# Expert blocks of different sizes, taken in falling order of tokens

## The chip, the cores and the metric

One NeuronCore of a Trainium2 chip runs the whole program. It has five engines with a queue each: PE (matrix multiply), DVE (vector), ACT (scalar and activation), POOL and SP. SP and ACT also issue the DMA transfers spoken of here. Each queue runs in the order written, and an instruction that waits for a semaphore holds up everything behind it on its engine. The metric is the device time of one execution in microseconds (us).

## What is computed

Three stages follow one another: a clustered attention (2 batches, 8 heads, 768 positions), a mixture of eight experts of which each token uses one, and a dense two-layer stage. The change is in the expert stage:

```
logits = x @ w_gate                        # x: 1536 x 512
expert_idx = argmax(logits, axis=1)        # one of 8 experts per token
for e in range(8):
    mask = expert_idx == e
    h = maximum(x[mask] @ w1[e], 0)        # 512 -> 1024
    out[mask] = gate_w[mask] * (h @ w2[e]) # 1024 -> 512
```

How many tokens an expert gets depends on the data. With the reference's inputs (its default seed) the counts are 198, 119, 169, 188, 162, 192, 206 and 302 for experts 0 to 7, worked out from the reference.

## The kernel before

The attention stage ends by scattering each token's row (512 numbers, its index and its gate) to a DRAM buffer `Xs`, which has a region of 1536 rows for each expert. Before that, SP fills the first rows of each region with zeros (line 687), so that a block may be read past its last token.

The expert stage runs in *blocks*. Block `blk` below 8 is expert `blk` with a fixed 208 rows (`CAP`), whatever its count. A ninth block of 128 rows (`OB`) takes the first rows that some expert has beyond 208; a table made on DVE at run time says which expert, which rows and where to put them (`table_a` to `table_e`). Any further such blocks run in a loop at lines 1049 to 1081, whose number of turns is a value read from SBUF. With the counts above, expert 7 alone has more than 208 rows (94 more), so the ninth block is used and the loop makes no turn.

A block is eight steps `f`, and a global step is `g = 8*blk + f`. In each step PE runs four matmuls of the first layer, `l1` (line 895), and four of the second, `l2` (line 911), the latter two steps behind (`LAG`). A group of four such products is eight instructions in the trace, since each 32-bit product is split in two; rows of the timeline show them as x8. The rows of the block are the moving operand, so a matmul's length grows with the rows of its block, and the weights of an expert are loaded in any case. ACT evacuates each `l1` group with a Relu (line 897) into `h`, and two PSUM banks alternate between the groups of `l1`: `l1` of step g+2 needs the Relu of step g to be done.

Each expert's weights are four chunks of 1 MB. A ring of four SBUF slots holds them, and SP issues the next block's chunk when the last matmul that reads its slot has run (`wload`, lines 126 to 131). The next block's rows are loaded from `Xs` by ACT (`x_load`, line 814) at f = 0, and PE turns them (`x_transp`, line 878) at f = 6, two quarters of the 512 columns to a PSUM bank; ACT and DVE copy the banks out.

Beside this runs the *conversion* of the third stage's weights from 64-bit to pairs of 32-bit halves: 32 pieces, each loaded by SP (0.5 MB into one of two `raw` buffers, line 150) and passed through ACT (`cv`, line 154), DVE (lines 159 to 162), ACT (line 169) and DVE (line 172). One conversion step (`conv_run`) does one part for each of five neighbouring pieces: ACT's part on piece k-1 waits for the load issued in the step before, and the load of piece k waits until DVE has consumed piece k-2. `conv_steps` decides in which global steps this happens: 22 of them spread evenly over the 72 steps of the expert stage, and one in each step of the third stage.

The loop at line 1050 also is a meeting point: all engines wait there for each other and SP for all its transfers, before the third stage begins with `x2_split` on ACT (line 1102).

Of the kernel before, what the change touches and what calls it, by code (L numbers as in the profile page):

```python
# [10 lines left out]
F32 = mybir.dt.float32  # L11
# [10 lines left out]
P = 128  # L22
# [5 lines left out]
N = B * S  # L28
# [5 lines left out]
OB = 128  # L34
XCOLS = N + CAP
XW = DM + 2
# [10 lines left out]
C_TOK = 402  # L47
C_END = 414


def make_consts():
    c = np.zeros((P, C_END), np.float32)
    p = np.arange(P)
    c[:, C_ID:C_ID + P] = np.eye(P)
    c[:, C_TRI:C_TRI + P] = p[:, None] < p[None, :]
    same = p[:, None] // NC == p[None, :] // NC
    c[:, C_FIRST:C_FIRST + P] = np.eye(P) - NC * (same & (p[:, None] < p[None, :]))
    c[:, C_TIE8:C_TIE8 + E] = E - np.arange(E)
    c[:, C_EBASE:C_EBASE + E] = N * np.arange(E)
    isk = (p // NC) % 2 == 1  # L60
    c[:, C_ESC] = np.where(isk, NEG, 1.0)
    c[:, C_ESC + 1] = np.where(isk, -NEG, 0.0)
    c[:, C_TOK:C_TOK + NT] = (p[:, None] + P * np.arange(NT)[None, :]).astype(np.int32).view(np.float32)
    return c


def make_table():


    t = np.zeros((NSEL, 3 * NOV + 1), np.float32)  # L70
# [9 lines left out]
def tile_cluster_attention_moe(ctx: ExitStack, tc: tile.TileContext, qk, kk, v, cen, cenr, gate, mw, m2w,  # L80
# [23 lines left out]
    off = const.tile([P, E], F32, name="off")  # L104
    offi = const.tile([1, E], I32, name="offi")
    ovi = const.tile([1, NSEL, 4], I32, name="ovi")


    NB = E + 1
    NCE = 4 * NB  # L110
# [3 lines left out]
    wslots, m2w_t = {}, {}  # L114
    ovr = {}
# [542 lines left out]
    for p in range(1, NPR):  # L658
# [148 lines left out]

    def halves(blk):
        return (2, CAP // 2) if blk < E else (1, OB)

    def x_load(blk, src):
        nt, np_ = halves(blk)
        xr = xrp.tile([P, 2, XW], F32, name=f"xr_{blk}", tag="xr")
        nc.scalar.dma_start(xr[0:np_, 0:nt, :], src.rearrange("(t p) d -> p t d", p=np_))
        xrt[blk] = xr
# [31 lines left out]
    placemm(rc, 0, False)  # L847
    x = xtp.tile([P, 4, CAP], F32, name="x_0", tag="x")
    for d in range(4):
# [17 lines left out]
    def x_transp(blk):  # L867
        nt, np_ = halves(blk)
        nb = nt * np_
        xr = xrt[blk]  # L870
        x = xtp.tile([P, 4, CAP], F32, name=f"x_{blk}", tag="x")[:, :, 0:nb]
        for g in range(2):
            ps = bank(2 + g)[:, 0:2 * nb]
            for k in range(2):
                d = 2 * g + k
# [3 lines left out]
            pv = ps.rearrange("p (d n) -> p d n", d=2)  # L879
            if g == 0:  # L880
                nc.scalar.activation(x[:, 0:2, :], pv, AF.Copy)
            else:
                nc.vector.tensor_copy(x[:, 2:4, :], pv)
        xts[blk] = x

    def l1(blk, f):
        nt, np_ = halves(blk)
        nb = nt * np_
        ci = 4 * blk + 2 * (f // 4)
# [12 lines left out]
    def l2(blk, f):  # L902
        nt, np_ = halves(blk)
        nb = nt * np_
        ci = 4 * blk + 2 * (f // 4) + 1
# [9 lines left out]
    def y_evac(blk, col):  # L915
        nt, np_ = halves(blk)
        nb = nt * np_
        for o, y in enumerate(yps.pop(blk)):
# [7 lines left out]
    sc = pool(moe, "sc")  # L926

    def offsets():
        t0 = sc.tile([P, E], F32, name="t0")
        t1 = sc.tile([P, E], F32, name="t1")  # L930
        nc.vector.memset(t0, 0.0)
        nc.vector.tensor_copy(t0[:, 1:E], cnt[:, 0:E - 1])
        a, bb = t0, t1
        for k, shf in enumerate((1, 2, 4)):
            dst = off if k == 2 else bb
            nc.vector.tensor_copy(dst[:, 0:shf], a[:, 0:shf])
            nc.vector.tensor_add(dst[:, shf:E], a[:, shf:E], a[:, 0:E - shf])
            a, bb = dst, a
        nc.vector.tensor_copy(offi, off[0:1, :])

# [45 lines left out]
    def table_e():  # L986
        nc.vector.tensor_scalar_add(ov[:, 2:3], ov[:, 2:3], float(N))
        nc.vector.tensor_scalar(ov[:, 3:4], sums["incl"][:, NOV - 1:NOV], -1.0, 0.0, ALU.add, ALU.max)
        nc.vector.tensor_copy(ovp, ov)
        nc.sync.dma_start(ovi, ovp)  # L990

    side = {2: [offsets], 11: [table_a], 13: [table_b], 16: [table_c], 18: [table_d], 20: [table_e]}

    def put_places(blk, c):
        nt, np_ = halves(blk)
        nc.sync.dma_start(PG[c, :].rearrange("(t p) c -> p t c", p=np_), xrt[blk][0:np_, 0:nt, DM:XW])
# [9 lines left out]

    KE = 22

    def conv_steps(g):
        if g < NG:  # L1010
            at_ = lambda g: max(0, g - 2) * KE // (NG - 2)
            return range(at_(g), at_(g + 1))
        g -= NG + LAG
        return range(KE + g, KE + g + 1) if g >= 0 else ()

    for g in range(NG + LAG):
# [11 lines left out]
        if g < NG:  # L1028
            if f == 0 and 1 <= blk + 1 < E:
                x_load(blk + 1, Xs[(blk + 1) * N:(blk + 1) * N + CAP, :])  # L1030
            if f == 2:
                if blk >= 1:
                    src = offi[0:1, blk:blk + 1] if blk < E else ovi[0:1, 0, 2:3]
                    nb = CAP if blk < E else OB
                    col[blk] = ds(reg(src, COMP, N), nb)
                    put_places(blk, ds(reg(src, [ET.SP], N), nb))
                else:
                    nc.sync.dma_start(PG[col[0], :], Xs[0:CAP, DM:XW])
                if blk + 1 == E:
                    x_load(blk + 1, Xs[ds(ovr["row"], OB), :])  # L1040
            if f == 6 and blk + 1 < NB:
                x_transp(blk + 1)
            if g == 27:
                ovr["w"] = reg(ovi[0:1, 0, 0:1], [ET.SP], 4 * (E - 1))
                ovr["row"] = reg(ovi[0:1, 0, 1:2], [ET.Activation], E * N - OB)
        conv_run(cvp, conv_steps(g))


    more = nc.values_load(ovi[0:1, 1, 3:4], min_val=0, max_val=NSEL - 1)
    with tc.For_i(0, more, 1):  # L1050
        rw = reg(ovi[0:1, 1, 0:1], [ET.SP], 4 * (E - 1))
# [11 lines left out]
        for f in range(8):  # L1063
# [138 lines left out]
def layout(inputs):  # L1202
# [7 lines left out]
    for pr in range(NPAIR):  # L1210
# [28 lines left out]
```

## Time and profile before

| | us |
|---|---|
| median of 3 runs (lowest, highest) | 747.85 (747.2, 751.29) |
| profiled execution, its own time | 746.16 |
| span of its trace | 744.4 |
| expert stage on PE, first `l1` to the end of the last `l2` | 268.97 to 471.55 |
| first matmul of the third stage | 474.87 |

The time around the span is 746.16 - 744.4 = 1.76 us. In the timeline a row is a run of like instructions on one engine: its start, its duration (until the last of them ends), and in brackets how long the engine had been idle and who released it. Matmuls overlap a little, so a group's real length is the distance between the starts of two groups and not its duration. Idle time of an engine other than the one that sets the end costs nothing by itself.

### The profile page before, as it was taken

To read this page: it belongs to the slowest core of one execution; us is meant where nothing else is said; L and a number is where in the kernel's file an instruction comes from. 1 tells how busy PE (TensorE), PEld (TensorE's weight loads), DVE (VectorE), ACT (ScalarE), POOL (GpSimd) and SP (SyncE) were. 2 spreads that over 40 slices of the span, in tenths; PEclk is the share of its full clock that TensorE was granted. 3 is DMA by queue.
4 is the path that set the end of the run, shared out by engine and by line. 5 is a ranking of instruction groups with operands and counts; after the bars stand their busy time and mean duration, and the time that the engine had idled before them with its cause. 6 is when DMAs were issued, how large, how long until landed. Compare 5 with 4: busy or idle time off the path is not lost. (4 is left out here: it accounts for less than half of the span.)

```text
span 744.4 us, 10754 instructions
## 1 busy us (share of the span) xinstructions
PE 719.0 (97%) x4102; PEld 592.5 (80%) x4102; DVE 417.2 (56%) x774; ACT 287.1 (39%) x599; POOL 64.1 (9%) x69
## 2 busy tenths in 40 slices
PE   8899999999999999999999999699999999999996
PEld 3666666666666799999999999588888888888885
DVE  6877767788876631352532425499945433544332
ACT  4867867857676312232232323333322111211111
POOL 5120120212300110000000000000002000020002
PEclk9999999999999999999999999999999999999999
DMA  9064584262530037799886977233101000010001
GB/s 295 24 198 109 215 303 104 117 166 55 139 76 1 29 110 264 217 274 250 280 265 200 306 223 251 53 113 112 58 0 57 0 1 1 0 57 1 0 1 56
DMA packets 25844, 92.74 MB, mean 125 GB/s; under 512 B 7156, under 2 KB 8703, under 8 KB 21055
## 3 DMA queue, kind: packets, MB, share of 16 engines
q1 hardware_dynamic: 20375, 75.41, 32.6%
q0 software_dynamic: 3216, 12.60, 4.9%
q10 hardware_dynamic: 2200, 4.03, 1.9%
q8 instruction: 33, 0.54, 0.3%
q14 instruction: 20, 0.16, 0.1%
HBM read 78.04 MB, written 9.74 MB: 118 GB/s over the span
## 5 line engine op out<-in xcount | busy, mean ns | idle before, releaser
L895 PE MATMUL PS<-x,w 128*128 128x208 f32 (+1 forms) x576 | 108.9, 332 | 2.2 <-ACT h L897 2.2
L911 PE MATMUL PS<-h,w 128*128 128x208 f32 (+1 forms) x576 | 108.6, 332 | 0.0
L1126 ACT ACTIVATE gh<-gg 128x512 fp32r<-128x512 f32 x48 | 30.4, 632 | 192.4 <-DVE gg L1125 192.4
L387 DVE TENSOR_REDUCE sm<-PS 128x1 f32<-128x768 f32 x96 | 91.9, 957 | 17.8 <-PE PS L381 14.3
L895 PEld LDWEIGHTS PS<-x,w 128*128 128x128 f32 x576 | 98.3, 190 | 2.4 <-ACT h L897 2.4
L397 ACT ACTIVATE P<-PS,sm 128x768 f32<-128x768 f32 x96 | 86.5, 901 | 31.6 <-DVE sm L387 31.5
L911 PEld LDWEIGHTS PS<-h,w 128*128 128x128 f32 x576 | 98.4, 190 | 0.0
L411 PEld LDWEIGHTS PS<-cst,P 128*128 128x128 f32 x576 | 63.4, 141 | 29.4 <-ACT P L397 17.3
L411 PE MATMUL PS<-cst,P 128*128 128x128 f32 x576 | 82.5, 278 | 3.1 <-ACT P L397 1.5
L1124 DVE TENSOR_SCALAR gg<-PS,alph 128x512 f32<-128x512 f32 x48 | 36.0, 750 | 78.1 <-PE PS L1116 78.1
L1114 PE MATMUL PS<-x2hi,w2h 128*128 128x512 f32 x192 | 75.5, 393 | 3.3 <-ACT x2hi L1102 3.3
L1115 PE MATMUL PS<-x2lo,w2h 128*128 128x512 f32 x192 | 75.4, 393 | 0.2 <-DVE x2lo L1103 0.2
L1116 PE MATMUL PS<-x2hi,w2l 128*128 128x512 f32 x192 | 75.4, 393 | 0.0
L1144 PE MATMUL PS<-w2l,gh 128*128 128x512 f32 x192 | 74.7, 389 | 0.0
L1145 PE MATMUL PS<-w2h,gl 128*128 128x512 f32 x192 | 74.7, 389 | 0.0
L1143 PE MATMUL PS<-w2h,gh 128*128 128x512 f32 x192 | 74.7, 389 | 0.0
L414 DVE COPY PT<-PS 128x384 f32<-128x384 f32 x96 | 53.0, 552 | 38.0 <-PE PS L411 37.9
L380 PE MATMUL PS<-KA,QA 128*128 128x512 f32 x192 | 73.6, 383 | 0.0
L420 PE MATMUL PS<-PT,V 128*64 128x384 f32 (+1 forms) x432 | 72.4, 462 | 0.0
L897 ACT ACTIVATE h<-PS 128x208 f32<-128x208 f32 (+1 forms) x72 | 23.9, 334 | 122.5 <-PE PS L895 114.6
L381 PE MATMUL PS<-KB,QB 96*128 96x512 f32 x192 | 61.8, 343 | 2.5 <-DMA KB<-KA 2.5
L413 ACT ACTIVATE PT<-PS 128x384 f32<-128x384 f32 x96 | 46.7, 487 | 32.1 <-PE PS L411 30.7
(159 smaller groups left out, 866.1 us busy)
## 6 DMA issues: line engine op xcount, KB each, us to landing
w<-in_mw SPq DMA_DIRECT2D x36, 1024.0 KB
raw<-in_m2w SPq DMA_DIRECT2D x32, 512.0 KB
R<-in_qk SPq DMA_DIRECT2D x7, 768.0 KB
KA<-in_kk POOLq DMA_DIRECT2D x7, 768.0 KB, 7.4
Xs<-in_zeros SPq DMA_DIRECT2D x8, 417.6 KB
xr<-Xs ACTq DMA_DIRECT2D x8, 417.6 KB
QA<-QB SPq DMA_DIRECT2D x16, 192.0 KB
V<-in_v SPq DMA_DIRECT2D x8, 384.0 KB
```

The source lines that it names most:

```text
L380: nc.tensor.matmul(ps[:, ks], st["QA"][:, hh, q0:q0 + P], st["KA"][:, hh, ks], start=True, stop=False)
L387: nc.vector.tensor_reduce(smt[s], psS[s % 2], AX.X, ALU.max, negate=True)
L397: nc.scalar.activation(Pt, psS[s % 2], AF.Exp, bias=smt.pop(s)[:, 0:1], accum_out=RS[:, tt, h:h + 1])
L411: nc.tensor.transpose(v4[:, kt // 3, kt % 3, :], Pt[:, kt * P:(kt + 1) * P], idf)
L895: nc.tensor.matmul(ps, w[:, d, fs], x[:, d, :], start=d == 0, stop=d == 3)
L911: nc.tensor.matmul(yps[blk][o][:, 0:nb], w[:, f % 4, o * P:(o + 1) * P], h, start=f == 0, stop=f == 7)
L1114: nc.tensor.matmul(ps, whi[:, d, fs], xhi[:, d, :], start=d == 0, stop=False)
L1115: nc.tensor.matmul(ps, whi[:, d, fs], xlo[:, d, :], start=False, stop=False)
L1116: nc.tensor.matmul(ps, wlo[:, d, fs], xhi[:, d, :], start=False, stop=d == 3)
L1143: nc.tensor.matmul(y, gh[:, c], whi[:, f % 4, :], start=f == 0, stop=False)
L1144: nc.tensor.matmul(y, gh[:, c], wlo[:, f % 4, :], start=False, stop=False)
L1145: nc.tensor.matmul(y, gl[:, c], whi[:, f % 4, :], start=False, stop=f == 15)
```

## The change

Eight blocks remain. Block 0 is still expert 0 with 208 rows. Blocks 1 to 7 are the other experts in falling order of their counts, with 306, 216, 200, 192, 176, 168 and 128 rows (`CAPS`), loaded as 2 or 3 parts (`PARTS`). Which expert that is, is known at run time only: `offsets` ranks the counts on DVE and leaves, per block, the number of the first weight chunk (`wi`) and the first row in `Xs` (`rowi`); SP and ACT read these into registers, and the loads of weights and rows take their address from them. `offsets` moves from step 2 to step 0, `x_load` from f = 0 to f = 1. Every row beyond a block's size goes through the loop, which now makes as many turns as there are such blocks of 128. A block over 256 rows turns one quarter of its columns per PSUM bank instead of two. The conversion steps get a table (`PER`): 3, 8, 4, 3, 2, 1, 0, 2 in blocks 0 to 7, 23 in all. The zero fill covers 306 rows of each region instead of 208.

```diff
-XCOLS = N + CAP
+CAPS = (CAP, 306, 216, 200, 192, 176, 168, 128)
+PARTS = (2, 3, 2, 2, 2, 2, 2, 1)
+CMAX = max(CAPS)
...
-    NB = E + 1
+    NB = E
...
     def wsrc(ci):
-        if ci < 4 * E:
+        if ci < 4:
             return mwf[ci]
-        return mwf[ds(ovr["w"] + (ci - 4 * E), 1)].rearrange("a p c -> p (a c)")
+        return mwf[ds(wreg[ci // 4] + ci % 4, 1)].rearrange("a p c -> p (a c)")
...
-                at(j0 + 4, "C", lambda e=e: nc.sync.dma_start(Xs[e * N:e * N + CAP, :], zeros))
+                at(j0 + 4, "C", lambda e=e: nc.sync.dma_start(Xs[e * N:e * N + CMAX, :], zeros))
...
+        dn = 2 if 2 * nb <= 512 else 1
+        for g in range(4 // dn):
+            ps = bank(2 + g % 2)[:, 0:dn * nb]
...
-            if g == 0:
-                nc.scalar.activation(x[:, 0:2, :], pv, AF.Copy)
+            if g % 2 == 0:
+                nc.scalar.activation(x[:, dn * g:dn * (g + 1), :], pv, AF.Copy)
             else:
-                nc.vector.tensor_copy(x[:, 2:4, :], pv)
+                nc.vector.tensor_copy(x[:, dn * g:dn * (g + 1), :], pv)
...
+        nc.vector.scalar_tensor_tensor(key, cnt, float(E), cs(C_KEY), ALU.mult, ALU.add)
+        nc.vector.tensor_tensor(bef, row(key), colm(key), ALU.is_gt)
+        nc.vector.tensor_reduce(rank, bef, AX.X, ALU.add)
+        nc.vector.tensor_tensor(at_, row(rank), colm(cs(C_IOTA)), ALU.is_equal)
+        nc.vector.tensor_tensor(tmp, at_, row(cs(C_IOTA)), ALU.mult)
+        nc.vector.tensor_reduce(ids, tmp, AX.X, ALU.add)
+        nc.vector.tensor_scalar(wi, ids[0:1, :], 4.0, None, ALU.mult)
+        nc.vector.tensor_scalar(rowi, ids[0:1, :], float(N), None, ALU.mult)
...
-    side = {2: [offsets], 11: [table_a], 13: [table_b], 16: [table_c], 18: [table_d], 20: [table_e]}
+    side = {0: [offsets], 11: [table_a], 13: [table_b], 16: [table_c], 18: [table_d], 20: [table_e]}
...
-    KE = 22
+    PER = (3, 8, 4, 3, 2, 1, 0, 2)
+    KE = sum(PER)
     def conv_steps(g):
         if g < NG:
-            at_ = lambda g: max(0, g - 2) * KE // (NG - 2)
-            return range(at_(g), at_(g + 1))
+            blk, f = divmod(g, 8)
+            at_ = lambda f: sum(PER[:blk]) + PER[blk] * f // 8
+            return range(at_(f), at_(f + 1))
...
-            if f == 0 and 1 <= blk + 1 < E:
-                x_load(blk + 1, Xs[(blk + 1) * N:(blk + 1) * N + CAP, :])
+            if f == 1 and blk + 1 < NB:
+                wreg[blk + 1] = reg(wi[0:1, blk + 1:blk + 2], [ET.SP], 4 * (E - 1))
+                row = reg(rowi[0:1, blk + 1:blk + 2], [ET.Activation], E * N - N)
+                x_load(blk + 1, Xs[ds(row, CAPS[blk + 1]), :])
...
-    more = nc.values_load(ovi[0:1, 1, 3:4], min_val=0, max_val=NSEL - 1)
+    more = nc.values_load(ovi[0:1, 0, 3:4], min_val=0, max_val=NSEL)
```

Two places show how this moves instructions. The first is ACT in the middle of block 1, where `h_3` to `h_5` are the Relu results of its steps 3 to 5, `cv<-raw` is the conversion part that waits for a load, and `w2h<-cv` the later one. Before:

```order
L897 ACTIVATE h_3_3011<-PS 128x208
L154 ACTIVATE cv_3028<-raw_2957 128x512
L897 ACTIVATE h_4_3036<-PS 128x208
L897 ACTIVATE h_5_3046<-PS 128x208
L897 ACTIVATE h_6_3073<-PS 128x208
```

And now:

```order
L911 ACTIVATE h_3_3108<-PS 128x306
L183 ACTIVATE w2h_2703<-cv_3058 128x512
L168 ACTIVATE cv_3128<-raw_3102 128x512
L911 ACTIVATE h_4_3136<-PS 128x306
L183 ACTIVATE w2h_2705<-cv_3100 128x512
L168 ACTIVATE cv_3148<-raw_3130 128x512
L911 ACTIVATE h_5_3156<-PS 128x306
```

A `cv<-raw` and a `w2h<-cv` stand now between each Relu of block 1 and the next, where one conversion part stood among four Relus.

The second is SP at the end of the expert stage, from the last 1 MB chunks of weights on: `raw` is a conversion load, `PG<-xr` writes the places of the block's tokens, TENSOR_LOAD and ISA read a value into a register and set an address. Before:

```order
L130 DMA w_4072<-in_mw 128x2048
L150 DMA raw_4086<-in_m2w 128x1024
L999 TENSOR_LOAD ovi
L999 ISA x2
L996 ISA
L996 DMA PG<-xr_3967 128x2
L150 DMA raw_4148<-in_m2w 128x1024
L150 DMA raw_4188<-in_m2w 128x1024
L1049 TENSOR_LOAD ovi
```

And now:

```order
L144 DMA w_4106<-in_mw 128x2048
L1027 TENSOR_LOAD offi
L1027 ISA x2
L1024 ISA
L1024 DMA PG<-xr_3989 128x2
L164 DMA raw_4162<-in_m2w 128x1024
L164 DMA raw_4212<-in_m2w 128x1024
L1075 TENSOR_LOAD ovi
```

One of the three conversion loads behind the last weight chunk has moved ahead, into the earlier blocks; the two that remain are those of block 7's two conversion steps.

## Rows read from the trace of the kernel before

**Rows 1.** Page, busy time, share of the span and instructions of each engine.
```profile
PE 719.0 (97%) x4102; PEld 592.5 (80%) x4102; DVE 417.2 (56%) x774; ACT 287.1 (39%) x599; POOL 64.1 (9%) x69
```
**Rows 2.** Timeline of PE, one expert block: start, duration, line, operation, shape, count.
```profile
378.85 0.88 PE L878 MATMUL PS<-cst,xr 104*128 104x104 f32 x8
379.57 1.59 PE L895 MATMUL PS<-x,w 128*128 128x208 f32 x8
...
382.40 1.57 PE L895 MATMUL PS<-x,w 128*128 128x208 f32 x8
...
402.81 1.59 PE L895 MATMUL PS<-x,w 128*128 128x208 f32 x8
```
**Rows 3.** Timeline of PE, the ninth block and the way into the third stage.
```profile
448.59 0.60 PE L878 MATMUL PS<-cst,xr 128*128 128x128 f32 x4
449.02 1.57 PE L895 MATMUL PS<-x,w 128*128 128x208 f32 x8
...
459.12 1.06 PE L911 MATMUL PS<-h,w 128*128 128x128 f32 x8
...
464.48 1.06 PE L911 MATMUL PS<-h,w 128*128 128x128 f32 x8
467.72 1.16 PE L895 MATMUL PS<-x,w 128*128 128x128 f32 x8 [2.18 <-ACT h L897]
468.71 2.84 PE L911 MATMUL PS<-h,w 128*128 128x128 f32 x24
474.87 0.50 PE L1114 MATMUL PS<-x2hi,w2h 128*128 128x512 f32 x1 [3.31 <-ACT x2hi L1102]
```
**Rows 4.** Timeline of ACT in the same stretch.
```profile
466.84 0.66 ACT L154 ACTIVATE cv<-raw 128x512 f32<-128x512 f32 x1 [4.88 <-DMA raw<-in_m2w]
467.40 0.43 ACT L897 ACTIVATE h<-PS 128x128 f32<-128x128 f32 x2
...
474.19 1.15 ACT L1102 ACTIVATE x2hi<-x2a 128x512 fp32r<-128x512 f32 x2 [2.54 <-SPq L1050]
```
**Rows 5.** Timeline of SP's DMA issues in the same stretch.
```profile
453.11 3.86 SPq L130 DMA_DIRECT2D w<-in_mw  x2
459.93 0.34 SPq L150 DMA_DIRECT2D raw<-in_m2w  x1
...
462.79 7.48 SPq L150 DMA_DIRECT2D raw<-in_m2w  x2
```
**Rows 6.** Windows: span; busy us of PE, PEld, DVE, ACT, POOL; PEclk, DMA share, GB/s.
```profile
409.00:432.00 23.00, 23.00 (x136) 22.96 (x136) 9.59 (x18) 7.16 (x17) 0.00 (x0) 1.00 0.92 303
...
452.00:472.00 20.00, 17.37 (x145) 16.99 (x143) 10.17 (x20) 6.60 (x18) 0.00 (x0) 1.00 0.64 199
...
476.00:480.00 4.00, 4.00 (x12) 3.17 (x11) 1.47 (x4) 0.38 (x1) 0.00 (x0) 0.57 0.23 7
```
**Rows 7.** Timeline of DVE, one conversion step, from its first instruction to its last.
```profile
459.78 0.68 DVE L172 TENSOR_TENSOR w2l<-cv,w2h 128x512 fp32r<-128x512 f32 x1
...
462.03 0.69 DVE L162 SCALAR_TENSOR_TENSOR cv<-raw,cv 128x512 int32<-128x512 int32 x1
```
**Rows 8.** Timeline of ACT and PE in block 0: load and turning of block 1's rows.
```profile
273.53 0.32 ACTq L814 DMA_DIRECT2D xr<-Xs  x1
...
285.87 0.88 PE L878 MATMUL PS<-cst,xr 104*128 104x104 f32 x8
```
**Rows 9.** Windows around the load of block 0's rows, issued alone at 262.81.
```profile
262.00:264.00 2.00, 1.59 (x15) 1.35 (x14) 0.85 (x7) 0.21 (x1) 0.00 (x0) 1.00 0.16 14
264.00:265.00 1.00, 0.71 (x11) 0.54 (x9) 0.97 (x5) 0.00 (x0) 0.00 (x0) 1.00 0.63 212
265.00:266.00 1.00, 0.31 (x2) 0.31 (x3) 0.64 (x5) 0.00 (x0) 0.00 (x0) 1.00 0.68 181
266.00:267.00 1.00, 1.00 (x7) 1.00 (x6) 0.00 (x0) 0.00 (x0) 0.00 (x0) 1.00 0.03 6
```
**Rows 10.** Page, DMA issues: the zero fill, and two windows after the first of them.
```profile
Xs<-in_zeros SPq DMA_DIRECT2D x8, 417.6 KB
...
44.00:50.00 6.00, 6.00 (x44) 3.97 (x42) 3.91 (x8) 4.46 (x10) 2.45 (x2) 1.00 1.00 397
50.00:56.00 6.00, 6.00 (x42) 3.85 (x40) 5.02 (x9) 4.79 (x11) 1.16 (x1) 1.00 0.04 17
```

More of the change, by code (lines that the diff above doesn't have):

```diff
@@ L34 @@
 OB = 128
-XCOLS = N + CAP
+CAPS = (CAP, 306, 216, 200, 192, 176, 168, 128)
+PARTS = (2, 3, 2, 2, 2, 2, 2, 1)
+CMAX = max(CAPS)
+XCOLS = N + CMAX
 XW = DM + 2
@@ L47 @@
 C_TOK = 402
-C_END = 414
+C_KEY = 414
+C_IOTA = 422
+C_CAPS = 430
+C_END = 438
 def make_consts():
@@ L63, in make_consts @@
     c[:, C_TOK:C_TOK + NT] = (p[:, None] + P * np.arange(NT)[None, :]).astype(np.int32).view(np.float32)
+    c[:, C_KEY:C_KEY + E] = E - 1 - np.arange(E)
+    c[:, C_KEY] = E * (N + 1)
+    c[:, C_IOTA:C_IOTA + E] = np.arange(E)
+    c[:, C_CAPS:C_CAPS + E] = CAPS
     return c
@@ L105, in tile_cluster_attention_moe @@
     offi = const.tile([1, E], I32, name="offi")
+    wi = const.tile([1, E], I32, name="wi")
+    rowi = const.tile([1, E], I32, name="rowi")
+    capx = const.tile([P, E], F32, name="capx")
     ovi = const.tile([1, NSEL, 4], I32, name="ovi")
-    NB = E + 1
+    NB = E
     NCE = 4 * NB
@@ L805, in tile_cluster_attention_moe, with parts @@
     xrt, xts, yps, hts = {}, {}, {}, {}
-    def halves(blk):
-        return (2, CAP // 2) if blk < E else (1, OB)
+    def parts(blk):
+        return PARTS[blk], CAPS[blk] // PARTS[blk]
     def x_load(blk, src):
-        nt, np_ = halves(blk)
-        xr = xrp.tile([P, 2, XW], F32, name=f"xr_{blk}", tag="xr")
+        nt, np_ = parts(blk)
+        xr = xrp.tile([P, 3, XW], F32, name=f"xr_{blk}", tag="xr")
         nc.scalar.dma_start(xr[0:np_, 0:nt, :], src.rearrange("(t p) d -> p t d", p=np_))
@@ L847, in tile_cluster_attention_moe @@
     placemm(rc, 0, False)
-    x = xtp.tile([P, 4, CAP], F32, name="x_0", tag="x")
+    x = xtp.tile([P, 4, CMAX], F32, name="x_0", tag="x")[:, :, 0:CAP]
     for d in range(4):
@@ L867, in x_transp @@
     def x_transp(blk):
-        nt, np_ = halves(blk)
+        nt, np_ = parts(blk)
         nb = nt * np_
         xr = xrt[blk]
[L871 to L875, printed above, removed]
+        x = xtp.tile([P, 4, CMAX], F32, name=f"x_{blk}", tag="x")[:, :, 0:nb]
+        dn = 2 if 2 * nb <= 512 else 1
+        for g in range(4 // dn):
+            ps = bank(2 + g % 2)[:, 0:dn * nb]
+            for k in range(dn):
+                d = dn * g + k
                 for t in range(nt):
@@ L895, in l1 @@
             nc.tensor.matmul(ps, w[:, d, fs], x[:, d, :], start=d == 0, stop=d == 3)
-        h = hp.tile([P, CAP], F32, name=f"h_{blk}_{f}", tag="h")[:, 0:nb]
+        h = hp.tile([P, CMAX], F32, name=f"h_{blk}_{f}", tag="h")[:, 0:nb]
         nc.scalar.activation(h, ps, AF.Relu)
@@ L902, in l2 @@
     def l2(blk, f):
-        nt, np_ = halves(blk)
-        nb = nt * np_
+        nb = CAPS[blk]
         ci = 4 * blk + 2 * (f // 4) + 1
@@ L915, in y_evac @@
     def y_evac(blk, col):
-        nt, np_ = halves(blk)
-        nb = nt * np_
+        nb = CAPS[blk]
         for o, y in enumerate(yps.pop(blk)):
@@ L928, in offsets @@
     def offsets():
[L929 to L939, printed above, removed]
+        e8 = lambda n: sc.tile([P, E], F32, name=n)
+        e64 = lambda n: sc.tile([P, E, E], F32, name=n)
+        row = lambda ap: ap.unsqueeze(1).broadcast_to([P, E, E])
+        colm = lambda ap: ap.unsqueeze(2).broadcast_to([P, E, E])
+        cs = lambda k: cst[:, k:k + E]
+        key, rank, ids, offs = e8("key"), e8("rank"), e8("ids"), e8("offs")
+        bef, at_, tmp = e64("bef"), e64("at"), e64("tmp")
+        nc.vector.scalar_tensor_tensor(key, cnt, float(E), cs(C_KEY), ALU.mult, ALU.add)
[6 more added lines that the diff above has]
+        nc.vector.tensor_scalar(rowi, ids[0:1, :], float(N), None, ALU.mult)
+        nc.vector.tensor_tensor(bef, bef, row(cnt), ALU.mult)
+        nc.vector.tensor_reduce(off, bef, AX.X, ALU.add)
+        nc.vector.tensor_tensor(tmp, at_, row(off), ALU.mult)
+        nc.vector.tensor_reduce(offs, tmp, AX.X, ALU.add)
+        nc.vector.tensor_copy(offi, offs[0:1, :])
+        nc.vector.tensor_tensor(at_, at_, colm(cs(C_CAPS)), ALU.mult)
+        nc.vector.tensor_reduce(capx, at_.rearrange("p s e -> p e s"), AX.X, ALU.add)
     tabr = sc.tile([NSEL, 3 * NOV + 1], F32, name="tabr")
@@ L957, in table_a @@
         ob = off[0:NSEL, :].unsqueeze(1).broadcast_to([NSEL, NSEL, E])
+        xb = capx[0:NSEL, :].unsqueeze(1).broadcast_to([NSEL, NSEL, E])
+        nc.vector.tensor_tensor(vje(tab[:, 0, :]), vje(tab[:, 0, :]), xb, ALU.add)
         nc.vector.tensor_tensor(vje(flag), cb, vje(tab[:, 0, :]), ALU.is_gt)
@@ L987, in table_e @@
         nc.vector.tensor_scalar_add(ov[:, 2:3], ov[:, 2:3], float(N))
-        nc.vector.tensor_scalar(ov[:, 3:4], sums["incl"][:, NOV - 1:NOV], -1.0, 0.0, ALU.add, ALU.max)
+        nc.vector.tensor_copy(ov[:, 3:4], sums["incl"][:, NOV - 1:NOV])
         nc.vector.tensor_copy(ovp, ov)
         nc.sync.dma_start(ovi, ovp)
-    side = {2: [offsets], 11: [table_a], 13: [table_b], 16: [table_c], 18: [table_d], 20: [table_e]}
+    side = {0: [offsets], 11: [table_a], 13: [table_b], 16: [table_c], 18: [table_d], 20: [table_e]}
     def put_places(blk, c):
-        nt, np_ = halves(blk)
+        nt, np_ = parts(blk)
         nc.sync.dma_start(PG[c, :].rearrange("(t p) c -> p t c", p=np_), xrt[blk][0:np_, 0:nt, DM:XW])
@@ L1071, in tile_cluster_attention_moe @@
                 nc.tensor.matmul(ps[:, 0:OB], w1[:, d, :], xT[:, d, :], start=d == 0, stop=d == 3)
-            hT = hp.tile([P, CAP], F32, name=f"ohT_{f}", tag="h")[:, 0:OB]
+            hT = hp.tile([P, CMAX], F32, name=f"ohT_{f}", tag="h")[:, 0:OB]
             nc.scalar.activation(hT, ps[:, 0:OB], AF.Relu)
@@ L1078, in tile_cluster_attention_moe @@
             nc.vector.tensor_copy((x2a if o < 2 else x2b)[:, o % 2, ds(rc, OB)], ys[o][:, 0:OB])
-        sh = op.tile([1, NSEL - 2, 4], I32, name="osh")
-        nc.vector.tensor_copy(sh, ovi[:, 2:NSEL, :])
-        nc.vector.tensor_copy(ovi[:, 1:NSEL - 1, :], sh)
+        sh = op.tile([1, NSEL - 1, 4], I32, name="osh")
+        nc.vector.tensor_copy(sh, ovi[:, 1:NSEL, :])
+        nc.vector.tensor_copy(ovi[:, 0:NSEL - 1, :], sh)
     moe.close()
```

35 lines of the change are left out of this document (14 added, 21 removed).

## Prediction

> **What bounds the kernel now.** I read the page first: PE is busy 97% of the span, DVE 56%, ACT 39% [rows 1]. So a term counts if it shortens PE's work or a gap in it. The change lies in the expert stage, so I read PE's timeline there. In a block of 208 rows nothing interrupts PE: from one block's first product to the next's is 402.81 - 379.57 = 23.24 us, of which the turning of the next rows takes 379.57 - 378.85 = 0.72, and 16 groups the rest, 22.52/16 = 1.407 each [rows 2]. In the ninth block a group of 128 rows takes (464.48 - 459.12)/6 = 0.893 [rows 3]. There PE has its only gaps: it should go on at 464.48 + 0.893 = 465.37 and goes on at 467.72, and from 471.55 (468.71 + 2.84) to 474.87 it waits for the third stage [rows 3]. The timelines of ACT and SP name the causes: ACT stood 4.88 us at a conversion part whose load, issued at 459.93 behind two weight chunks, came at 466.84, with the Relus queued behind it [rows 4, 5]; and at the meeting point ACT waited 2.54 us for SP, whose last load was issued as late as about 469.9 (462.79 + 7.48 - 0.34) [rows 4, 5].
>
> **The sum, part by part.** *Rows of the blocks.* A line through the two measured groups gives 0.893 + 0.00643 (n - 128) us for n rows: 1.46 at 216, 1.36 at 200, 1.30 at 192, 1.20 at 176, 1.15 at 168. For 306 it gives 2.04, proportion to 208 gives 2.07; I take 2.05. Sixteen groups each: 22.5 + 32.8 + 23.3 + 21.7 + 20.9 + 19.2 + 18.4 + 14.3 = 173.1 us. Before it was 8 x 22.5 + 14.3 = 194.4. Gain 21.3, sure to about 0.5. All of it lies on PE, which waits for nothing in the blocks of 208.
>
> *Turning.* Eight turns of 104 rows take 0.72, so 0.087 us per 100 rows and turn; before 7 x 0.72 + 0.43 (449.02 - 448.59) = 5.5 [rows 2, 3]. Now block 1 has 12 turns of 102 rows (1.1), the others 0.4 to 0.75, together 4.8. Gain 0.7. Block 1's third quarter needs the PSUM bank of the first, which ACT must have copied out: two quarters of turns take 0.5 us, the copy about as long (a 512-wide ACT pass takes 0.66 [rows 4]). I charge 0.5 for it; it can cost nothing or, twice, 1.3.
>
> *The ninth block's gap.* Blocks 6 and 7 have 0 and 2 conversion steps, and no weight chunk is issued behind a block-7 load. The gap of 2.35 goes; it could come back only elsewhere (first rival).
>
> *Into the third stage.* The last conversion load before the meeting point can be issued when DVE has consumed the load two before, whose ACT part now ran four steps earlier, so at the start of step 7 at the latest, four groups or 3.6 us before PE's end, against 471.55 - 469.9 = 1.6 before. SP's wait then ends about 2 us sooner. But the engines also wait for each other there, so between nothing and 2.0 comes back; I take 0.6, nearer the low end, since loading the loop's count and the branches stay.
>
> *The clock after it.* From 476 to 480 the granted clock is 0.57, so (1 - 0.57) x 2 x 4 = 3.4 us at 1.2 instead of 2.4 GHz, a loss of 1.7 [rows 6]. Before it fell PE had stood still 3.3 us; after the 2.35 us of the ninth block the window shows it unchanged at 1.00 [rows 3, 6]. The gap that I expect, 2.7, lies between. I leave the loss in (the gap into the third stage is followed by thin work); the other end is 1.7 less.
>
> *Edits at nothing.* Ranking: `offsets` is 14 short DVE instructions instead of 9 at the start of block 0. Even at the 0.68 of a 512-wide one [rows 7], the eight before `rowi` take 5.4 us; the load that waits for them was held until 273.53 anyway and its rows are first read at 285.87 [rows 8]. The Relus of steps 0 and 1 now stand ahead of that load, not behind. Register reads on SP and ACT lie in waits that they have anyway. Weights: the tightest chunk is the last one, for block 7's second half, with nine groups, 8.0 us, from its slot's release to its use. Before, the corresponding chunk was issued by 456.97 (453.11 + 3.86) and used at 464.48 without a wait, in 7.5, with conversion loads beside it [rows 3, 5]; so nothing. Traffic: block 1 needs 4 MB of weights, 4 MB of conversion and 0.4 of rows in 34 us, 258 GB/s; before, PE ran 23 us without a gap at 303 GB/s and a share of 0.92 [rows 6]. Zero fill: 417.6 x 98/208 = 197 KB more per expert, two at a time 0.4 MB, 1 us at the 397 GB/s of the window in which they run; the 6 us after it are free (share 0.04) and PE is full in both [rows 10]. So nothing; 4 x 1 us if that cover failed.
>
> Together: -21.3 - 0.7 + 0.5 - 2.35 - 0.6 = -24.45. The profiled execution took 746.16, so 721.7. The shown runs lie at 747.2 to 751.29, median 1.7 above the profiled one; I add half of that distance and forecast **722.6**.
>
> **Rivals.** *First: ACT is held by conversion loads in block 1.* Eight steps of conversion now stand in eight steps of PE work, one between each pair of Relus. With two buffers, a load can follow the one two before only after its landing L, ACT's part (0.66), DVE's step (462.03 + 0.69 - 459.78 = 2.94) and the issue (0.34) [rows 4, 5, 7]: (L + 3.9)/2 per step, against 2 x 2.05 = 4.1 on PE. L was 6.9 behind two weight chunks (459.93 to 466.84), and at most 4.3 for the last load with none ahead (469.9 to 474.19). With 4.3 it just keeps up; with 6.9 it falls back 1.3 us per step, 10.4 in eight. A Relu may be late by one group and one step less the work before it, 6.15 - 1.1 = 5.05, before PE stops. So the cost is between nothing and 10.4 - 5.05, about 5.3. One chunk passes for every two loads, so I take L near 5, a lag of 2.8 and no stop. For the rival: the ninth block shows just this, 2.35 lost. Against: there the steps were groups of 0.893, with little slack. It gives about 728.
>
> *Second: block 1's rows come late.* Block 0's load, 417.6 KB in two parts of 104 rows, kept the DMA engines busy for 2 x 0.16 + 0.63 + 0.68 + 0.03 = 1.66 us of all sixteen, never above a share of 0.68 in a window, as if some engines took no part; it was over by about 267, so some 2.2 us beyond 2 of transfer [rows 9]. If 102-row parts spread over fewer engines, six say, the 614 KB take 2 x (306/208) x (13/6) = 6.4 us, and with 2.2 the rows are there at 282.1; they are wanted at 285.9 [rows 8]. Weight chunks on the same engines could double the transfer, to 288.5: 2.7 late, about 725. For it: the load's shape is new. Against: 3.8 us to spare.
>
> The Trainium skill, in DMA: Bandwidth & Descriptors, "Why a DMA increments its semaphore by 16 and not by 1", has a rule behind this: a transfer uses the largest number of engines up to 16 that divides its slowest dimension, so 13 for 104 parts and 6 for 102. The share below 13/16 in the windows agrees; no run before shows a 102-row load. By it the sum stays as it is unless the weights interleave as said; by bytes alone the rows would be there at 278.8.
>
> *Third, on the other side: the loop runs.* If one rank has a single row more than its block (say 193 for the block of 192), a turn of the loop loads eight pairs of quarter-megabyte weights through two buffers, each pair only after the last was used: 8 x (4.3 to 6.9 for landing + 2 x 0.893), plus one landing for the rows, 53 to 76 us, by the landings of twice that size above. Even at 53 the kernel takes 722.6 + 53 = about 776, slower than before. It decides from the first row over. Against: the reference's counts in falling order, 198 first, then 302, 206, 192, 188, 169, 162, 119, all fit, the tightest by 4; for it, that the trace before can't show the counts, only that no more than one block of 128 was over 208.
>
> **How the numbers follow.** Forecast as worked out 66%, first rival 20%, second 7%, loop 3%, and 4% for something unseen in the register-addressed loads that eats half of the gain or more. The range goes from 722.6 - 1.7 (clock) - 1.4 (rest of the meeting point) - 0.5 (groups), about 719, to 722.6 + 5.3 + 1.3, about 729; it leaves out the loop and the unseen. A difference under 0.5% (3.7 us) can't be told from none here. Faster 94%, same 2%, slower 4%.
>
> **What would show it.** Right: PE's groups in block 1 at 2.05 us and no gap in PE from block 0 to block 7; the meeting point's gap at about 2.7 instead of 3.31; the stage's end some 24 us earlier, the attention stage unchanged. Wrong: PE waiting for a Relu in block 1 or 2 while ACT waits for `raw` (first rival), PE waiting for a DMA before block 1's turns (second), instructions of the loop's body in the trace (third), or groups that do not shrink in proportion to their rows.

## The result, and the profile after

The changed kernel takes 721.02 us, median of 4 runs (720.69 to 727.78); the kernel before took 747.9 beside it (747.2 to 751.29). The ratio is 0.9655, 95% interval 0.9601 to 0.9709. The profiled execution took 720.73, its span 718.9. The forecast was 722.6, range 719 to 729.

The expert stage is compared on PE, from its first product to the first product of the third stage. Before: 268.97 to 474.87, 205.90 us. After: 268.90 to 451.01, 182.11. So 23.8 of the span's 25.5 us come from the stretch that the change edits. The rest, 1.6, came behind it: from the third stage's first product to the end 744.4 - 474.87 = 269.5 before, 718.9 - 451.01 = 267.9 after.

First the page's line of engine times (busy us, share of the span, instructions), which answers [rows 1]: PE is as full as before, with 24.5 us less to do.

```profile
PE 694.5 (97%) x3970; PEld 560.5 (78%) x3970; DVE 418.5 (58%) x779; ACT 283.3 (39%) x589; POOL 64.1 (9%) x69
```

PE's timeline after, at the places that answer [rows 2, 3, 8]: the turning of block 1's rows, two groups of 306, a group of block 2 that starts late, the last block, and the way into the third stage.

```profile
285.80 0.69 PE L893 MATMUL PS<-cst,xr 102*128 102x102 f32 x6
286.75 0.80 PE L893 MATMUL PS<-cst,xr 102*128 102x102 f32 x6 [0.26 <-ACT x L896]
287.38 1.59 PE L909 MATMUL PS<-x,w 128*128 128x208 f32 x8
...
299.22 2.22 PE L924 MATMUL PS<-h,w 128*128 128x306 f32 x8
301.28 2.23 PE L909 MATMUL PS<-x,w 128*128 128x306 f32 x8
...
339.92 1.62 PE L924 MATMUL PS<-h,w 128*128 128x216 f32 x8
341.49 1.73 PE L909 MATMUL PS<-x,w 128*128 128x216 f32 x8
...
442.19 1.06 PE L909 MATMUL PS<-x,w 128*128 128x128 f32 x8
443.58 1.16 PE L924 MATMUL PS<-h,w 128*128 128x128 f32 x8 [0.33 <-DMA w<-in_mw]
444.57 1.06 PE L909 MATMUL PS<-x,w 128*128 128x128 f32 x8
...
451.01 0.49 PE L1140 MATMUL PS<-x2hi,w2h 128*128 128x512 f32 x1 [2.70 <-ACT x2hi L1128]
```

A group of 306 rows takes 301.28 - 299.22 = 2.06 (forecast 2.05). Block 1's turns take 287.38 - 285.80 = 1.58 with the wait for ACT's copy in the middle (forecast 1.1 + 0.5). The gap of the ninth block is gone, and the gap into the third stage is 2.70 instead of 3.31. Two small stops are new: a product that should start at 442.19 + 0.89 = 443.08 starts at 443.58, with the last weight chunk, and one that should start at 339.92 + 1.46 = 341.38 starts at 341.49, with a Relu that ACT began only at 341.12.

ACT's timeline at the meeting point answers the second row of [rows 4]. The wait there no longer names SP; what is left, 1.92 us, shows no releaser in the profile.

```profile
450.33 1.15 ACT L1128 ACTIVATE x2hi<-x2a 128x512 fp32r<-128x512 f32 x2 [1.92 <-issue]
```

And the window that answers [rows 6] (columns as there; the third number from the end is the granted clock, PEclk): it stays at 1.00 behind the gap.

```profile
450.00:456.00 6.00, 4.76 (x20) 3.72 (x21) 3.90 (x7) 2.19 (x4) 0.00 (x0) 1.00 0.14 2
```

### The profile page after: what moved, and what is told of

It reads as the page before. It is cut to its first block, busy times and chain, and to the rows that moved or that the text cites. A ratio compares the mean times of both kernels' runs of the same rounds, so it can differ in the third digit from the quotient of the medians.

```text
span 718.9 us, 10539 instructions
## 1 busy us (share of the span) xinstructions
PE 694.5 (97%) x3970; PEld 560.5 (78%) x3970; DVE 418.5 (58%) x779; ACT 283.3 (39%) x589; POOL 64.1 (9%) x69
## 5 line engine op out<-in xcount | busy, mean ns | idle before, releaser
L909 PE MATMUL PS<-x,w 128*128 128x208 f32 (+7 forms) x512 | 96.9, 332 | 0.0
L924 PE MATMUL PS<-h,w 128*128 128x208 f32 (+7 forms) x512 | 96.6, 332 | 0.3 <-DMA w<-in_mw 0.3
L924 PEld LDWEIGHTS PS<-h,w 128*128 128x128 f32 x512 | 83.7, 190 | 4.9 <-DMA w<-in_mw 0.5
L909 PEld LDWEIGHTS PS<-x,w 128*128 128x128 f32 x512 | 83.7, 190 | 4.5 <-ACT h L911 0.3
L911 ACT ACTIVATE h<-PS 128x208 f32<-128x208 f32 (+7 forms) x64 | 21.1, 332 | 78.1 <-PE PS L909 76.2
```

What stands on the lines that cost most here:

```text
L924: nc.tensor.matmul(yps[blk][o][:, 0:nb], w[:, f % 4, o * P:(o + 1) * P], h, start=f == 0, stop=f == 7)
```

## Experiments

Single executions of one kernel differ by some 10 us. The experiments are therefore read from the stretch defined above (the "stage" from here on: 182.11 after, 205.90 before), with the times beside it. The expectations count the expert stage only to the end of the last block's last product, without the gap into the third stage, which is 2.7 us less after and 3.3 before (by the rows 179.4 and 202.6, where they have 179.2 and 202.3).

**The changed kernel twice more**, unaltered, once in each of two sets of runs.

> The changed kernel once more, unaltered, as the measure for the runs beside it, whose differences lie under 1%. 721 us by every theory; the granted clock after the third stage's first products stays at 1.00 if a gap of 2.7 us does not make it fall, and shows 0.5 for about 3.4 us in executions near 722.5 if it sometimes does.

> The changed kernel once more as the measure for these rounds: expert stage on PE 179.0 to 179.5, gap into the third stage 2.70. If the granted clock's fall after that gap is not set by its length, it falls in some executions and not in others, and the third stage to the end takes 269.3 or 267.9.

Measured: 724.28 (720.95 to 728.48, 6 runs) against 748.85, ratio 0.9667 [0.9622, 0.9713]; and 724.46 (721.85 to 731.15, 6 runs) against 748.88, ratio 0.9705 [0.9657, 0.9754]. The stage takes 182.30 and 181.56, so it repeats to 0.7 us. The first of the two, PE's timeline and a window:

```profile
286.59 1.57 PE L924 MATMUL PS<-h,w 128*128 128x208 f32 x8
288.74 0.74 PE L893 MATMUL PS<-cst,xr 102*128 102x102 f32 x6 [0.59 <-DMA xr<-Xs]
...
453.39 0.63 PE L1140 MATMUL PS<-x2hi,w2h 128*128 128x512 f32 x1 [2.70 <-ACT x2hi L1128]
```
```profile
452.00:458.00 6.00, 4.51 (x12) 3.33 (x13) 2.50 (x4) 2.19 (x4) 0.00 (x0) 0.72 0.15 3
```

Two things follow. The gap of 2.70 is the same as in the first profile, and here the clock falls to its lower level behind it. In the eleven profiles in which that gap was 2.58 to 2.70, the clock fell in eight and stayed in three; the third stage to the end takes 269.1 to 269.6 us in the one case and 267.9 to 268.0 in the other. What decides between them stays open. And PE did wait here for block 1's rows: the second rival, at 0.59 us.

**Block 1's rows in parts of 104 and of 101.**

```
-CAPS = (CAP, 306, 216, 200, 192, 176, 168, 128)
+CAPS = (CAP, 312, 216, 200, 192, 176, 168, 128)     # c_312
+CAPS = (CAP, 303, 216, 200, 192, 176, 168, 128)     # d_303
```

> Block 1 of 312 rows in three parts of 104 instead of 306 in three of 102. Theory (a part's rows decide how many DMA engines carry it: 13 for 104, 6 for 102): 6 rows more cost 16 x 6 x 0.00643 = 0.6 us on PE, so 721.6; the last of the block's rows lands some 4 us earlier than the 284.83 of the changed kernel, with increments from 13 engines instead of 6. Rival (the load takes its 11.3 us because it waits behind weight chunks and conversion loads, whatever its shape): it lands at 284 or later, time also about 721.6.

> Block 1 of 303 rows in three parts of 101 instead of 306 in three of 102: 0.3 us less for PE's groups, and 1% fewer bytes to load. Theory (a transfer uses the largest number of engines up to 16 that divides a part's rows: 13 for 104, 6 for 102, one for 101): the rows' load, 11.3 to 13.6 us with 6 engines and 6.1 with 13, is left to one engine; 608 KB there take 30 us or more, and PE waits for them 15 us or more before block 1's turns (the wait named DMA xr), so the time is 736 or more. Rival (the load waits behind others and its shape hardly counts): it lands within 1 us of the changed kernel's and the time is 721 to 724.

Measured: 312 rows 723.48 (722.5 to 724.74), ratio 0.9653 [0.9616, 0.9691], stage 181.92; 303 rows 755.33 (751.01 to 757.55) against 748.54, ratio 1.0075 [1.0049, 1.0102], stage 210.05. Three rows fewer make the kernel slower than the one before, by under 1%. PE's timeline of the kernel with 303, and two windows of it:

```profile
290.70 1.57 PE L924 MATMUL PS<-h,w 128*128 128x208 f32 x8
317.16 2.61 PE L893 MATMUL PS<-cst,xr 101*128 101x101 f32 x12 [24.89 <-DMA xr<-Xs]
```
```profile
295.00:317.00 22.00, 0.00 (x0) 0.00 (x0) 0.00 (x0) 0.00 (x0) 0.00 (x0) 0.50 0.07 26
317.00:323.00 6.00, 5.83 (x24) 5.33 (x25) 3.09 (x6) 1.20 (x4) 0.00 (x0) 0.55 0.01 3
```

All engines stand still while the rest of the 608 KB arrives at 26 GB/s with a DMA share of 0.07, about one sixteenth; when PE goes on, its granted clock is 0.55, near its lower level. By the trace's records of completions the load took 6.06 us in parts of 104, 11.29 in parts of 102 (10.3 to 13.6 in the other profiles with them), 37.55 in parts of 101, and raised its semaphore 14, 7 and 2 times. So the shape of a part sets the load's length, and the rival (it merely queues behind others) is out. The Trainium skill's rule in DMA: Bandwidth & Descriptors, "Why a DMA increments its semaphore by 16 and not by 1" (the largest number up to 16 that divides the slowest dimension: 13, 6, 1 engines) agrees with the order, and with the counts too: one increment of each load stands 0.58 to 0.77 us after its issue, and the others, 13, 6 and 1, come 5.6 to 6.1, 9.7 to 11.3 and 37.55 us after it.

**The conversion's steps: spread evenly, and pressed together.**

```
-    PER = (3, 8, 4, 3, 2, 1, 0, 2)
+    PER = (3, 3, 3, 3, 3, 3, 3, 2)     # c_conv_even
+    PER = (1, 12, 4, 2, 2, 1, 0, 1)    # d_conv12
```

> The conversion's 23 steps spread evenly over the blocks (3 each, 2 in the last) instead of 8 in the block of 306 rows and 0 in that of 168. Theory (raw loads hold ACT only where steps are dense, and the last blocks' weight chunks are the tight transfers): block 1 loses its 9.3 us for two steps and ACT's waits for raw there nearly go, but nothing of that was on PE's path; the loads now stand beside the weight chunks of the short blocks, so PE waits for weights or for Relus there, 0.5 to 4 us more: 721.5 to 725. Rival one (the order of the conversion makes no difference because all of its cost is hidden either way): 721, within 0.5. Rival two (block 1's dense steps cost something on PE): up to 1 us less, 720.

> Twelve of the 23 conversion steps stand in block 1 instead of eight, fewer in blocks 0, 3, 4, 5 and 7. Theory (two raw buffers let a step take 4.6 to 4.9 us there, the first rival of the prediction, which was held off only by ACT's slack of 5.05): twelve steps take 55 to 59 us against block 1's 33 on PE; ACT falls behind by more than its slack after about the seventh step, and PE stops for Relus (the wait named ACT h) in block 1 for some 10 to 18 us in all: 731 to 740. Rival (the loads only seem slow because ACT comes to them late, and quicken when pressed): PE stops for under 3 us, 721 to 725.

Measured: even 722.28 (720.66 to 728.32), ratio 0.9657 [0.9611, 0.9703], stage 181.88; twelve 739.09 (736.55 to 745.14, 4 runs), ratio 0.9867 [0.9799, 0.9935], stage 193.89, 11.8 more than the changed kernel's. ACT's waits for raw loads from 285 to 335 us (total, count, longest), first of the changed kernel, then of the even table, and PE's stops with twelve steps:

```profile
ACT cv L168 <- DMA raw<-in_m2w: 25.0, 9, 6.7
```
```profile
ACT cv L168 <- DMA raw<-in_m2w: 4.3, 2, 2.8
```
```profile
312.64 2.33 PE L909 MATMUL PS<-x,w 128*128 128x306 f32 x8 [1.15 <-ACT h L911]
...
324.93 3.47 PE L909 MATMUL PS<-x,w 128*128 128x306 f32 x8 [3.78 <-ACT h L911]
...
337.75 1.73 PE L909 MATMUL PS<-x,w 128*128 128x216 f32 x8 [1.86 <-ACT x L896]
...
348.12 1.73 PE L909 MATMUL PS<-x,w 128*128 128x216 f32 x8 [3.05 <-ACT h L911]
```

With eight steps ACT stands 25 us of 50 for raw loads and PE hardly notices; with twelve PE stops four times, 9.8 us in all, three times for a Relu and once for ACT's copy of the turned rows. (The steps come out of blocks 0, 3 and 7; 4 and 5 keep theirs.) The first stop came earlier than expected, at ACT's third conversion part of the block and not after the seventh step. ACT's first and twelfth conversion part with twelve steps:

```profile
301.63 0.67 ACT L168 ACTIVATE cv<-raw 128x512 f32<-128x512 f32 x1 [2.74 <-DMA raw<-in_m2w]
...
347.16 0.66 ACT L168 ACTIVATE cv<-raw 128x512 f32<-128x512 f32 x1 [2.55 <-DMA raw<-in_m2w]
```

That is (347.16 - 301.63)/11 = 4.1 us a step, where I had expected 4.6 to 4.9: as the rival in the second of these expectations says, the loads come somewhat quicker when pressed, but not enough to spare PE. So the first rival's mechanism is real; the change stands just on the harmless side of it, and not in every execution. Among the eight profiles with eight steps in block 1, four show no named stop for a Relu (the changed kernel's own three, and 312), the others 0.49 (tighter sizes, below), 0.92 (sizes of 208, below), 1.48 (303) and 2.35 in three stops (the loop, below). Four of these six stops stand in block 2, beside the table's four steps there and not its eight. The even table lost its expected 0.5 to 4 us nowhere in the stage: my theory that the short blocks' weight chunks would suffer fell. Rival one (all of it hidden either way) fits; rival two's gain of up to 1 us can't be told from it, since the unaltered kernel's stage itself lies between 181.56 and 182.30. The even table's profile has no stop for a Relu.

**Sizes alone, back and further.**

```
-CAPS = (CAP, 306, 216, 200, 192, 176, 168, 128)
+CAPS = (CAP, 306, 208, 208, 208, 208, 208, 208)     # d_sizes208, two parts in the last block
+CAPS = (CAP, 306, 208, 192, 192, 176, 168, 120)     # c_tight
```

> Blocks 2 to 7 go back to 208 rows each; block 0, block 1 (306 rows), the conversion table and the missing ninth block stay: 168 rows more than the changed kernel. Theory (a row costs PE 16 x 0.00643 us, wherever it stands): 17.3 us more, the expert stage on PE 179.2 + 17.3 = 196.5, the time about 739 to 742. Rival (part of the changed kernel's gain is that short blocks overlap better, or part of it is lost again to weight chunks in the short blocks): the difference is off by 1 us or more from 17.3, less if the short blocks wait for weights.

> Blocks of 306, 208, 192, 192, 176, 168 and 120 rows instead of 306, 216, 200, 192, 176, 168 and 128: 24 rows less. Theory (PE's rows set the time, 16 x 0.00643 us each): 2.5 us less, about 718.5. Rival (ACT held by conversion loads, or the last weight chunks, has used up the slack of the shorter groups): the gain shrinks to 1 us or less, and PE's gap before the last groups for the weight chunk, 0.33 us now, grows. If a block is too small for its rank's rows, the loop runs and the time rises by over 50 us; the reference's counts in falling order (302, 206, 192, 188, 169, 162, 119) say that it does not.

Measured: 208s 742.48 (738.73 to 748.94, 10 runs), ratio 0.9923 [0.9887, 0.996], stage 200.63; tighter 722.55 (720.23 to 728.81), ratio 0.9651 [0.9603, 0.9698], stage 180.27, 2.0 less than the unaltered kernel beside it. The 208s cost 18.5 us against the 17.3 worked out from the rows alone. In the profile of the 208s a Relu is late once, behind a conversion part in block 2 (rows below; the product should start at 345.74 + 1.41 = 347.15 and starts at 348.23), which is 1.1 of it.

```profile
345.74 1.57 PE L924 MATMUL PS<-h,w 128*128 128x208 f32 x8
348.23 1.67 PE L909 MATMUL PS<-x,w 128*128 128x208 f32 x8 [0.92 <-ACT h L911]
```
```profile
347.28 0.66 ACT L168 ACTIVATE cv<-raw 128x512 f32<-128x512 f32 x1 [6.05 <-DMA raw<-in_m2w]
```

That 17.3 and 1.1 nearly make 18.5 is in part chance. The changed kernel's own timeline gives a group of 168 rows 1.14 us:

```profile
424.84 1.30 PE L924 MATMUL PS<-h,w 128*128 128x168 f32 x8
425.98 1.30 PE L909 MATMUL PS<-x,w 128*128 128x168 f32 x8
```

From 168 to 208 rows (1.407) a row therefore costs a group 0.0067, and not the 0.0064 of the line drawn from 128. By the spacings of that timeline (1.46, 1.35, 1.30, 1.19, 1.14 and 0.89 for blocks 2 to 7) the rows make 16 x (6 x 1.407 - 7.34) = 17.6. The longer turns add 0.5 and the late Relu 1.1; the 0.6 of stops in the changed kernel's profile and 0.1 of its longer gap go off: 18.5. So rows and turns explain it, and nothing is left for the rival that short blocks overlap better or worse.

**One turn of the loop.**

```
-CAPS = (CAP, 306, 216, 200, 192, 176, 168, 128)
+CAPS = (CAP, 306, 216, 176, 192, 176, 168, 128)
```

> Block 3's size goes from 200 to 176 rows, below the 192 of the fourth largest rank, so the loop makes one turn for its further rows. Theory (third rival of the prediction): 24 rows fewer save 2.5 us, and one turn costs 53 to 76 us: 771 to 798. Rivals: the turn's weights stream faster than the landings suggest, since nothing else loads then: 735 to 760; or the loop's branches and its register loads cost more than its loads: over 800.

Measured: 765.18 (760.89 to 766.3, 4 runs), ratio 1.0186 [1.0132, 1.0239]; stage 222.35. PE's timeline: the last block's end, the loop's first and last products, the third stage.

```profile
446.67 2.84 PE L924 MATMUL PS<-h,w 128*128 128x128 f32 x24
450.24 0.44 PE L1086 MATMUL PS<-cst,oxr 128*128 128x128 f32 x2 [0.72 <-DMA oxr<-Xs]
...
451.65 1.16 PE L1097 MATMUL PS<-oxT,ow 128*128 128x128 f32 x8
...
485.84 2.07 PE L1097 MATMUL PS<-oxT,ow 128*128 128x128 f32 x8 [0.69 <-DMA ow<-in_mw]
489.06 2.05 PE L1101 MATMUL PS<-ohT,ow 128*128 128x128 f32 x8 [1.15 <-DMA ow<-in_mw]
492.75 0.80 PE L1140 MATMUL PS<-x2hi,w2h 128*128 128x512 f32 x1 [1.64 <-ACT x2hi L1128]
```

From the end of the last block to the third stage it takes 492.75 - 449.51 = 43.2 us instead of 2.7. A turn costs about 40.5, not 53 to 76: the third rival's sign was right and its price too high. The time lies between the theory's 771 and the 760 of the run's first rival, faster loads. A step takes (485.84 - 451.65)/7 = 4.9 us, where I had at least 6.1, because by the completion records the loop's quarter-megabyte loads, alone on the queues, took 2.4 to 4.0 us; and this although PE ran the loop's second half at the lower clock (a group there lasts 2.07 instead of 1.16).

**The ninth block's gap by itself**, in the kernel before.

```
-            at_ = lambda g: max(0, g - 2) * KE // (NG - 2)
+            at_ = lambda g: min(KE, max(0, g - 2) * KE // (NG - 10))
```

> The kernel before, with its conversion steps of the expert stage all in the first eight blocks and none in the ninth; sizes, ninth block and loop stay as they were. Theory (the ninth block's gap was ACT held by a raw load behind two weight chunks, and part of the wait into the third stage was a late last load): the gap of 2.35 goes, so the expert stage on PE takes 202.3 - 2.35 = 199.9, and the gap into the third stage goes from 3.31 to 2.7: 3 us in all, about 745 against 748. Rival one (the stop is the ninth block's own weight chunks; the conversion is blamed for it): the stage stays at 202. Rival two (the steps, closer together now, hold ACT elsewhere): new stops named ACT h in the blocks of 208, which give part of it back.

Measured: 744.33 (743.57 to 752.21, 12 runs) against 748.88, ratio 0.995 [0.9917, 0.9983]; stage 202.83, 3.07 less than before. PE's timeline at the ninth block's end and into the third stage, to be laid beside [rows 3]:

```profile
465.72 1.06 PE L895 MATMUL PS<-x,w 128*128 128x128 f32 x8
466.62 1.06 PE L911 MATMUL PS<-h,w 128*128 128x128 f32 x8
...
471.98 2.84 PE L911 MATMUL PS<-h,w 128*128 128x128 f32 x24
477.51 0.49 PE L1114 MATMUL PS<-x2hi,w2h 128*128 128x512 f32 x1 [2.70 <-ACT x2hi L1102]
```

Both terms come as worked out: no gap between the groups of 128, 2.70 into the third stage, and no stop named ACT h in the blocks of 208 (rival two). The ninth block's own weights weren't to blame, and 3.0 of the change's 24 us are a matter of where the conversion stands, to be had without any ranking.

**Tighter sizes and a nearly even table together.**

```
-CAPS = (CAP, 306, 216, 200, 192, 176, 168, 128)
+CAPS = (CAP, 306, 208, 192, 192, 176, 168, 120)
-    PER = (3, 8, 4, 3, 2, 1, 0, 2)
+    PER = (3, 4, 4, 3, 3, 3, 2, 1)
```

> The tighter sizes (24 rows fewer) and a nearly even conversion table (3, 4, 4, 3, 3, 3, 2, 1). Theory (each row 16 x 0.00643 us; the conversion's steps cost nothing when spread, and the stops of up to 0.6 us for late Relus or weight chunks go): an expert stage on PE of 179.2 - 2.5 - 0.3 = 176.4, and a time about 2.5 us under the changed kernel's in the same rounds, 718.5 to 721. Rival (the shorter last block leaves its weight chunks too little time once conversion steps lie beside them): a wait named DMA w of 0.5 us or more in the last two blocks, and a stage of 177 or more.

Measured: 721.8 (721.25 to 725.46, 6 runs), ratio 0.965 [0.9612, 0.9688], beside 724.46 of the changed kernel in the same set; stage 179.52, 2.0 less. PE shows no wait for a Relu or a weight chunk from block 0 to the end of the last. It is the best stage seen; in whole executions the two kernels' intervals overlap. In the expectation's measure that is 179.5 - 2.7 = 176.8, where it had 176.4 and the rival 177 or more. The gain in the stage is below the 2.5 to 2.8 expected, and the last block says why: groups of 120 rows in PE's timeline.

```profile
440.58 1.06 PE L909 MATMUL PS<-x,w 128*128 128x120 f32 x8
441.47 1.06 PE L924 MATMUL PS<-h,w 128*128 128x120 f32 x8
442.37 1.06 PE L909 MATMUL PS<-x,w 128*128 128x120 f32 x8
```

A group of 120 takes 0.89, just as one of 128; the 8 rows cut from the last block, priced at 0.8 us, bring nothing. The line of cost against rows ends above 128 already: from 1.14 at 168 rows, 0.0067 a row, it would reach 0.87 at 128, and meets 0.89 at about 131 rows, an estimate from these groups.

## Why the prediction was right

- **Rows of the blocks, -21.3: right.** 306 rows 2.06, 216 rows 1.46 (341.38 - 339.92 by the unhindered spacing); by the spacings of all sizes 16 x (8 x 1.407 + 0.893 - 1.407 - 2.06 - 7.34) = 21.5. The line was drawn through a group of 128, which is already at the floor, so its 0.00643 a row is a little low; at these sizes that is 0.2 us in all. Shown also by undoing it: 168 rows back cost 18.5, of which the rows make 17.6.
- **Turning, -0.7, and the bank wait, +0.5: right.** Block 1's turns took 1.58 against 1.6.
- **The ninth block's gap, -2.35, and the way into the third stage, -0.6: right,** each shown alone in the kernel before (3.07 together against 2.95). I had allowed up to 2.0 at the meeting point; SP's wait did go, but 1.92 us with no visible releaser remained, and 2.70 stood in nearly every kernel whose last conversion load came early.
- **The clock after it: left in, and in the first profile not lost.** The forecast chose one outcome of something that goes either way at the same gap. I had made it hang on the gap's length between 2.35 and 3.3; the runs don't bear that out, since 2.70 did both.
- **Edits at nothing: nearly.** The tightest weight chunk, which I costed at nothing from its 7.5 us before, took longer than its 8.0 in the first profile (8.3 by the completion records) and stopped PE by 0.50; in the two repeats (5.7 and 6.5) it did not. Ranking, zero fill and register reads show no stop.
- **The sum.** The stage fell by 23.79 where the terms make 24.45; the difference is that 0.50, the 0.11 of the late Relu, and roundings.
- **First rival, given 20%: the mechanism is there, mostly without its price.** L came out near the 5 that I took: by the completion records the eight loads of block 1 landed after 4.2 to 7.2 us, 5.1 on average. SP's timeline of the changed kernel agrees, by the first raw load of block 1 and the one eight loads later:

```profile
290.38 4.16 SPq L164 DMA_DIRECT2D raw<-in_m2w  x2
...
327.08 0.33 SPq L164 DMA_DIRECT2D raw<-in_m2w  x1
```

  (327.08 - 290.38)/8 = 4.6 us a step, so L = 2 x 4.6 - 3.9 = 5.3. Against 4.1 a step on PE that used up most of ACT's slack, and four of eight profiles show 0.5 to 2.4 us of stops, in block 1 or 2.
- **Second rival, 7%: closer than I priced it.** I had the rows there at 282.1; they landed at 284.83 with 0.97 to spare, and in one repeat 0.59 late. The number of engines was right; that loads beside it would stretch it, from 8.6 us by this estimate to 11.3 (10.3 to 13.6 in the others), was in the rival only.
- **Third rival: right in sign, price 40 instead of 53 to 76.**
- **The range.** All 16 runs of the changed kernel lie between 720.69 and 731.15, two of them over 729; the median over all is 723.6. The first four runs have a median of 721.02, 2.6 lower, and single executions differ by 10 us; that the forecast came within 1.6 us of that median is in part luck. The terms are borne out by the stage, which repeats to 0.7. What differs most between profiles lies ahead of the change, and I had left it out: the stage starts at 268.8 to 271.4 in some profiles and at 274.6 to 275.2 in others. The windows from 72 to 84 us show where, first of a late start (the tighter sizes with the nearly even table), then of an early one (the second repeat); the row between them is PE's wait in the first.

```profile
72.00:84.00 12.00, 9.82 (x47) 5.79 (x48) 3.66 (x5) 4.28 (x9) 3.57 (x2) 0.72 1.00 373
```
```profile
75.51 0.76 PE L394 MATMUL PS<-KA,QA 128*128 128x512 f32 x1 [2.18 <-DMA QA<-QB]
```
```profile
72.00:84.00 12.00, 12.00 (x85) 8.18 (x84) 8.80 (x13) 9.37 (x19) 3.62 (x2) 1.00 0.99 399
```

With the DMA engines full, PE waits 2.18 us for a transfer in the attention stage and then runs at the lower clock. All five profiles with a late start have this wait, 2.2 to 2.4 us, and none of the eight with an early one has it. The kernel before with its conversion moved is among the five (2.27 at 76.46), so the wait does not need the change.

## What to carry to other kernels

When PE is full, price a change in rows by the measured spacing of its groups, and look for the size below which that spacing stops shrinking. When a table moves background work, compare the period of that work (landing and the work that frees its buffers) with the period of the work it stands beside, and keep the slack in mind: ACT waiting half of the time cost next to nothing here, and four steps more cost 12 us. And check the shape of every new transfer: parts of 101 rows instead of 102 turned a gain of 25 us into a loss.

## What the runs showed of the hardware that I had not expected

- A load of three parts of 101, 102 or 104 rows took 37.55, 11.29 and 6.06 us for about the same 608 to 626 KB.
- At the same gap of 2.70 us ahead of the third stage the granted clock fell in some executions and not in others, and with it 1.2 to 1.7 us came or went.
- A group of eight products with 120 columns took as long as with 128 (0.89 us), while from 168 to 306 rows each further row cost 0.0067.
